# A 64-column rest unit in the first expert stage, and five moves around VectorE

## The chip, the cores and the metric

One core of a Trainium2 chip runs the kernel. Its TensorE (PE in the profile) multiplies, ScalarE (ACT) and VectorE (DVE) read PSUM and write SBUF, GpSimd (POOL) masks and scatters, SyncE (SP) issues most DMAs. The metric is the device time of one execution in microseconds; smaller is better.

## The reference

Decayed attention over 8 batches of 576 tokens, then two mixtures of experts, each of which sends every row to one of 8 experts:

```python
x = np.ascontiguousarray(attn_out.transpose(0, 2, 1, 3)).reshape(B * S, H * D)   # 4608 x 512
# both mixtures: e_idx = argmax(x @ w_gate [+ modality_bias])
for e in range(E):
    mask = e_idx == e
    h = np.maximum(x[mask] @ w1[e], 0.0)          # 512 -> 1024
    out[mask] = weight[mask, None] * (h @ w2[e])  # 1024 -> 512
```

Counting with the reference's own seeded inputs, the first mixture sends 602, 613, 589, 549, 586, 487, 608 and 574 rows to experts 0 to 7.

## The kernel before

The kernel has three parts. *Attention* (a written plan of times, `PLAN`, sorted and issued in that order) makes 36 chunks of 128 tokens, routes them, and scatters each row to its expert's place in DRAM. *Stage 1* walks the 8 experts of the first mixture in order, *stage 2* the 8 of the second. There each engine has its own stream of instructions with branches on register values, and the engines meet only at semaphores.

An expert's rows come in units. A pair unit has 256 rows, and alternates between slot 0 and slot 1; what is left over, up to 128 rows, is the *rest unit*. The number of pairs (`np`) and the kind of rest (`od`) are read from the row counts into registers of every engine. In stage 1 `od` is 0 (no rest) or 2 (a rest of 128 rows, though it may hold fewer); in stage 2 it can be 1, too, for a rest of at most 64 rows, which TensorE then multiplies with `SMALL`, 64 columns.

On TensorE a unit is the *first product* (`ph`, four quarters of 24 matmuls, lines 1136 to 1138, a weight load before each) and then, block of 128 rows by block, the *second product* (`py`, 24 matmuls of 512 columns a block, lines 1144 to 1146). The weights are two f16 numbers each, so each product is three. After each quarter of the first product ScalarE writes `max(ph, 0)` to `hT` in f16 (line 1264) and VectorE what f16 lost of it (the *rest of h*, line 1388); the second product takes `h_full` four times, once for each quarter. After the second product each block goes *back*: ScalarE squares `py` (1249), VectorE makes a scale from the sum (`eb`, `v_s`), ScalarE scales (1252), VectorE writes the low half of the row (`x2row`).

Between these lies the routing for the second mixture, some units late: TensorE makes logits (`L1114`), VectorE *chooses* (six small instructions from `w_L` to `oh`), TensorE counts ranks from `oh` (`L1119`, `L1120`; it waits for `oh_full`), VectorE *places* (`v_gq`, `w_pr`, `cum`). `routed` sets after which quarter each is done: in slot 0 a block is chosen at quarter 0 and its ranks are counted after quarter 2 of the first product, and another chosen at quarter 2 with its ranks after the first quarter of the second product.

The next expert's weights come as four staged megabytes; of each a `conv` on ScalarE (1238, about 1.9 us) makes the high half, and one on VectorE (`wb<-stg`, about 2.29 us) the low half. TensorE takes `w_full` for two of them before an expert's first product, for the other two before its second product in slot 0. For expert 1 the four are converted inside expert 0 and, the last on VectorE, in slot 0 of expert 1. VectorE's small work all has line 559, since one helper (`Chain`) issues it; each result that others wait for is told by waits that VectorE's sequencer runs one after another. `ahead` loads `np` and `od` of the next expert into the engine's registers.

Of the kernel before, what the change touches and what calls it, by code (L numbers as in the profile page):

```python
# [13 lines left out]
F32 = mybir.dt.float32  # L14
I32 = mybir.dt.int32
AF = mybir.ActivationFunctionType
ALU = mybir.AluOpType
# [75 lines left out]
def attention_and_routing(tc, st, I, K):  # L93
# [328 lines left out]

    def enough():

        pm = ps.tile([P, 512], F32, tag="pl", name="pm_enough")
        nc.tensor.matmul(pm[:, 0:8], ones, held[0], start=True, stop=True)
        nc.vector.tensor_copy(K["reg1"][:, 24:25], pm[0:1, 0:1])

# [40 lines left out]
    def counts():  # L469

        pm = total[0]
        cf = one.tile([1, 8], F32, tag="cf", name="cf")
        c2 = one.tile([1, 1, 8], I32, tag="c2", name="c2")
        reg = K["reg1"]
        nc.vector.tensor_copy(reg[:, 16:24], pm[0:1, 0:8])
        nc.vector.tensor_tensor(cf, pm[0:1, 0:8], col("eR")[0:1], op=ALU.subtract)
        nc.vector.tensor_scalar(c2[:, 0], cf, 127.0, None, op0=ALU.add)
        nc.vector.tensor_scalar(reg[:, 0:8], c2[:, 0], 8, None, op0=ALU.logical_shift_right)
        nc.vector.tensor_scalar(reg[:, 8:16], c2[:, 0], 6, 2, op0=ALU.logical_shift_right, op1=ALU.bitwise_and)


    fetch, high, low = first_weights(nc, I, K, lambda m: two.tile([P, 1024], F32, tag="w0s", bufs=4, name=f"w0s{m}"))
# [91 lines left out]
def experts(nc, st, I, K, out):  # L574
# [159 lines left out]
                unit(P_, 1, PAIR, True)  # L734
                eng.reg_add(i, i, 1)

    def walk(co, R_, P_, unit, none=None, conv=None, first=None, late=None, opening=None, owed=None):

        eng, pairs, od = co.eng, R_["np"][P_ % E], R_["od"][P_ % E]
        if P_ < E:  # L740
            block, after = co.label("block"), co.label("after")

            def without():
                if none:
                    none()
                if first and P_ == 0:
                    first()
                if owed:
                    owed()
                for k in range(2 if conv and P_ == 0 else 0):  # L750
                    conv(1, k)
                if conv and P_:
                    for slot in range(2):
                        for q in range(2):
                            brought(eng, R_, P_, conv, slot, q)

            def other():
                with when(eng, pairs, "GT", 1):
                    unit(P_, 1, PAIR, True, 1)
                    pairs_from(eng, R_, P_, unit, 2)  # L760
                if conv:
                    with eng.Else():
                        for k in range(2) if P_ == 0 else ():
                            conv(1, k)
                        for q in range(2) if P_ else ():
                            brought(eng, R_, P_, conv, 1, q)
            if opening and P_ == 0:
                opening(without)
            else:
                co.unlikely(pairs, "LT", 1, without, block)  # L770
                unit(P_, 0, PAIR, False, 0)
            co.unlikely(pairs, "NE", 2, other, block)
            unit(P_, 1, PAIR, True, 1)
            co.to(block)
            if late:
                co.unlikely(od, "EQ", 0, late, after)
            else:
                co.jump(od, "EQ", 0, after)
            unit(P_, 2, FULL, False)
            co.to(after)  # L780
            return
        with when(eng, pairs, "GT", 0):
            unit(P_, 0, PAIR, False, 0)
            with when(eng, pairs, "GT", 1):
                unit(P_, 1, PAIR, True, 1)
                pairs_from(eng, R_, P_, unit, 2)
        if none:
            with eng.Else():
                none()
        with when(eng, od, "EQ", 2):  # L790
            unit(P_, 2, FULL, False)
        with eng.Else():
            with when(eng, od, "EQ", 1):
                unit(P_, 2, SMALL, False)
        if conv:
            rest(eng, R_, P_, conv)
# [58 lines left out]
    with nc.Block() as block:  # L855
# [245 lines left out]
        def _(pe):  # L1101
            with ExitStack() as rs:
# [89 lines left out]
                for P_ in range(NP):  # L1192
                    if P_ == E:
                        take(pe, "w_full", 4)
                        with when(pe, R_["early"], "GT", 0):
                            for k in range(EP):
                                unit(E, k, PAIR, False, routing=k == 0, counting=k == 0)
                        with pe.Else():
                            routed(pe, was, 0, False, None, lambda b: (logits(b), ranks(b)))
                            counts(cum)  # L1200
                        take(pe, "reg_pe")
                        less_early(pe, R_)
                    co.leave(R_, P_)
                    if P_ and P_ != E:
                        take(pe, "w_full", 2)

                    def none(P_=P_):
                        if P_ not in (0, E):
                            take(pe, "w_full", 2)
                        coming(P_)  # L1210
                        if P_ == E - 2:
                            counts(cums)
                    def opening(without):

                        def slow():
                            count1(pe, R_, 0)
                            with when(pe, R_["np"][0], "LT", 1):
                                without()
                            with pe.Else():
                                ready(READY)  # L1220
                                unit(0, 0, PAIR, False, 0)
                        go = co.label("go")
                        co.unlikely(R_["known"], "LT", PAIR, slow, go)
                        unit(0, 0, PAIR, False, 0, made=True)
                        count1(pe, R_, 0)
                        co.to(go)
                    walk(co, R_, P_, unit, none, opening=opening)
                co.end()

        @block.scalar  # L1230
        def _(ac):
            with ExitStack() as rs:
# [24 lines left out]
                def unit(P_, s, w, sure, slot=None, routing=None):  # L1257
# [13 lines left out]
                    if opening:  # L1271
                        go = co.label("go")
                        co.unlikely(R_["known"], "LT", PAIR, relus, go)
                        co.to(go)
                    else:
                        relus()
                        if slot == 0:
                            brought(ac, R_, P_, conv, slot, 1)
                        for k in (2, 3) if (P_, s) == (0, 2) else ():
                            conv(1, k)  # L1280
                    ac.sem_inc(T[f"x_free{s}"])
                    for b in range(blocks[s]):
                        back(P_, s, b)
                    if P_ < E:
                        note(ac, was, s, sure)

# [4 lines left out]
                for P_ in range(NP):  # L1291
# [9 lines left out]
                        less_early(ac, R_)  # L1301
                    co.leave(R_, P_)
                    ahead(ac, R_, P_)
                    walk(co, R_, P_, unit, conv=conv, late=(lambda: [conv(1, k) for k in (2, 3)]) if P_ == 0 else None)
                co.end()

        @block.vector
        def _(ve):
            ch = Chain(ve, T, "dve")
            tt, ts, stt, tr = ve.tensor_tensor, ve.tensor_scalar, ve.scalar_tensor_tensor, ve.tensor_reduce  # L1310
            with ExitStack() as rs:
# [66 lines left out]
                def unit(P_, s, w, sure, slot=None, routing=None):  # L1378
# [3 lines left out]
                    def rests():  # L1382
                        for g in range(4):
                            routes = routing or behind(P_, slot)
                            if routes and g < 3:
                                routed(ve, was, s, sure, g, choose, 2)
                            take(ve, "hh_full")
                            stt(hT[:, 1, 2 * g:2 * g + 2, cs], ph[g][:, :, cs], 0.0, hT[:, 0, 2 * g:2 * g + 2, cs], op0=ALU.max, op1=ALU.subtract).then_inc(T["h_full"])  # L1388
                            if routes:
                                if g == 3:  # L1390
                                    routed(ve, was, s, sure, g, choose, 2)
                                if (P_, s, g) == (E - 2, 2, 3):
                                    order()
                                if (P_, s, g) == (0, 2, 3):
                                    conv(1, 2)
                                if slot == 0 and g == 3:
                                    brought(ve, R_, P_, conv, 0, 0)
                                routed(ve, was, s, sure, g, place, 2)
                            if P_ and slot == 1 and g == 1:
                                brought(ve, R_, P_, conv, slot, 0)  # L1400
                            if (P_, slot, g) == (0, 1, 1):
                                conv(1, 0)
                            if (P_, slot, g) == (1, 0, 1):
                                conv(1, 3)
                    if opening:
                        go = co.label("go")
                        co.unlikely(R_["known"], "LT", PAIR, rests, go)
# [80 lines left out]
                for P_ in range(NP):  # L1488
# [13 lines left out]
                            final_counts()  # L1502
                        less_early(ve, R_)
                    co.leave(R_, P_)
                    ahead(ve, R_, P_)

                    def none():
                        ve.sem_inc(T["cnt_ask"])
                        totals()
                    walk(co, R_, P_, unit, none if P_ == E - 2 else None, conv, nothing, {0: lambda: conv(1, 2), E - 2: order}.get(P_),  # L1510
                         owed=(lambda: conv(1, 3)) if P_ == 1 else None)
                co.end()

        @block.gpsimd
# [135 lines left out]
```

## Time and profile before

| | us |
|---|---|
| median of 3 runs | 987.47 (987.39 to 988.93) |
| the profiled execution | 986.25 |
| its span, first to last instruction | 984.5 |
| TensorE busy in it | 964.9 (98%) |
| VectorE, ScalarE busy | 437.1 (44%), 353.8 (36%) |

Busy is the time with at least one instruction in flight, so a share of 98% says that TensorE is seldom seen waiting, not that its array runs at its peak. Times in the rows count from the span's start. Attention lasts until about 181, stage 1 until 594, stage 2 to the end.

### The profile page before, as it was taken

To read this page: it belongs to the slowest core of one execution; us is meant where nothing else is said; L and a number is where in the kernel's file an instruction comes from. 1 tells how busy PE (TensorE), PEld (TensorE's weight loads), DVE (VectorE), ACT (ScalarE), POOL (GpSimd) and SP (SyncE) were. 2 spreads that over 40 slices of the span, in tenths; PEclk is the share of its full clock that TensorE was granted. 3 is DMA by queue.
4 is the path that set the end of the run, shared out by engine and by line. 5 is a ranking of instruction groups with operands and counts; after the bars stand their busy time and mean duration, and the time that the engine had idled before them with its cause. 6 is when DMAs were issued, how large, how long until landed. Compare 5 with 4: busy or idle time off the path is not lost. (4 is left out here: it accounts for less than half of the span.)

```text
span 984.5 us, 25261 instructions
## 1 busy us (share of the span) xinstructions
PE 964.9 (98%) x9218; PEld 684.2 (69%) x9218; DVE 437.1 (44%) x1402; ACT 353.8 (36%) x699; POOL 213.1 (22%) x301
## 2 busy tenths in 40 slices
PE   8999998999999999999999999999999999999997
PEld 6888887666676766767775776776666667766664
DVE  4676677366656565656566663243111211121111
ACT  4665565235444352434453432232111111211111
POOL 6677765011111111111111111100010101000110
PEclk9999999999999999999999999999999999999999
DMA  9999992578376664748664852642221311112101
GB/s 349 375 337 328 330 303 111 121 216 235 75 194 139 150 189 122 196 110 236 121 184 97 235 161 61 215 87 44 55 60 36 76 35 55 43 43 64 54 21 36
DMA packets 170070, 145.20 MB, mean 147 GB/s; under 512 B 135081, under 2 KB 135245, under 8 KB 169936
## 3 DMA queue, kind: packets, MB, share of 16 engines
q1 hardware_dynamic: 160928, 114.85, 43.0%
q0 software_dynamic: 8960, 28.62, 7.8%
q8 instruction: 73, 1.20, 0.5%
q14 instruction: 61, 0.50, 0.2%
q10 hardware_dynamic: 48, 0.04, 0.0%
HBM read 80.46 MB, written 33.92 MB: 116 GB/s over the span
## 5 line engine op out<-in xcount | busy, mean ns | idle before, releaser
L1138 PE MATMUL ph<-xT,wb 128*128 128x256 f16 (+2 forms) x1312 | 329.3, 262 | 0.0
L1137 PE MATMUL ph<-xT,wb 128*128 128x256 f16 (+2 forms) x1312 | 329.3, 262 | 0.0
L1136 PE MATMUL ph<-xT,wb 128*128 128x256 f16 (+2 forms) x1312 | 329.2, 262 | 0.0
L1388 DVE SCALAR_TENSOR_TENSOR hT<-ph,hT 128x512 f16<-128x512 f32 (+2 forms) x164 | 103.2, 636 | 322.0 <-DVEq L547 321.2
L1144 PE MATMUL py<-wb,hT 128*128 128x512 f16 x608 | 230.3, 379 | 0.1
L1146 PE MATMUL py<-wb,hT 128*128 128x512 f16 x608 | 230.4, 379 | 0.0
L1145 PE MATMUL py<-wb,hT 128*128 128x512 f16 x608 | 230.4, 379 | 0.0
L1264 ACT ACTIVATE hT<-ph 128x512 f16<-128x512 f32 (+2 forms) x164 | 90.1, 550 | 175.8 <-ACTq L547 175.6
L1136 PEld LDWEIGHTS ph<-xT,wb 128*128 128x128 f16 x1312 | 128.2, 98 | 15.6
L1137 PEld LDWEIGHTS ph<-xT,wb 128*128 128x128 f16 x1312 | 128.2, 98 | 15.4
L1138 PEld LDWEIGHTS ph<-xT,wb 128*128 128x128 f16 x1312 | 128.3, 98 | 12.2
L1146 PEld LDWEIGHTS py<-wb,hT 128*128 128x128 f16 x608 | 59.4, 98 | 71.8
L1551 POOL DMA_INDIRECT out_dram<-yo,idxo x37 | 35.9, 970 | 334.5 <-POOLq L547 324.7
L1144 PEld LDWEIGHTS py<-wb,hT 128*128 128x128 f16 x608 | 59.3, 98 | 64.3 <-issue 0.9
L1145 PEld LDWEIGHTS py<-wb,hT 128*128 128x128 f16 x608 | 59.4, 98 | 63.2
L559 DVE SCALAR_TENSOR_TENSOR wb<-stg,wb 128x2048 f16<-128x2048 f32 x36 | 82.4, 2288 | 10.0 <-DVEq L547 9.0
L1255 ACT ACTIVATE yo<-py,v_gcol 128x512 f32<-128x512 f32 x37 | 25.4, 687 | 167.5 <-ACTq L547 167.5
L1540 POOL TENSOR_SCALAR idx<-v_pos 128x1 int32<-128x1 f32 x39 | 9.1, 232 | 335.0 <-POOLq L547 335.0
L1238 ACT ACTIVATE wb<-stg 128x2048 f16<-128x2048 f32 x36 | 68.4, 1901 | 0.9 <-ACTq L547 0.9
L1249 ACT ACTIVATE sq<-py 128x512 bf16<-128x512 f32 x39 | 23.3, 596 | 93.4 <-ACTq L547 93.4
L1544 POOL DMA_INDIRECT xs<-x2row,idx x39 | 43.3, 1111 | 37.8 <-POOLq L547 36.5
L332 POOL TENSOR_SCALAR_AFFINE_SELECT a<-a 128x512 f32<-128x512 f32 x64 | 39.5, 641 | 26.2 <-ACT a L326 25.3
(165 smaller groups left out, 946.5 us busy)
## 6 DMA issues: line engine op xcount, KB each, us to landing
stg<-in_moe_w_dram SPq DMA_DIRECT2D x36, 1024.0 KB
dq<-in_dq_dram SPq DMA_DIRECT2D x34, 512.0 KB
vk<-in_vk_dram SPq DMA_DIRECT2D x30, 512.0 KB
w0s<-in_moe_w_dram SPq DMA_DIRECT2D x8, 512.0 KB
xs<-zero SPq DMA_DIRECT2D x8, 262.0 KB, 2.3
xs<-zero SPq DMA_DIRECT2D x8, 258.0 KB
vk<-in_vk_dram SPq DMA_DIRECT2D x8, 256.0 KB
gx<-in_scales_dram SPq DMA_DIRECT2D x5, 256.0 KB
```

The lines of the kernel that those rows point to most:

```text
L332: nc.gpsimd.affine_select(out=d4, in_=d4, pattern=[[0, 4], [1, C]], compare_op=ALU.is_ge, fill=0.0, base=0, channel_multiplier=-1)
L559: r = fn(*a, **kw).then_inc(self.sem, 1)
L1136: pe.matmul(o, w1(P_, 0)[:, c, fs], xT[s][:, c, cs], start=(c == 0), stop=False)
L1137: pe.matmul(o, w1(P_, 0)[:, c, fs], xT[s][:, 4 + c, cs], start=False, stop=False)
L1138: m = pe.matmul(o, w1(P_, 1)[:, c, fs], xT[s][:, c, cs], start=False, stop=(c == 3))
L1144: pe.matmul(py[b], hT[:, 0, f, bs], w2(P_, 0)[:, f, :], start=(f == 0), stop=False)
L1145: pe.matmul(py[b], hT[:, 0, f, bs], w2(P_, 1)[:, f, :], start=False, stop=False)
L1146: m = pe.matmul(py[b], hT[:, 1, f, bs], w2(P_, 0)[:, f, :], start=False, stop=(f == 7))
L1238: ac.activation(wb[P_ % 2][:, 0, 2048 * c:2048 * c + 2048], stg[:, 2048 * c:2048 * c + 2048], AF.Copy, scale=WS).then_inc(T["cv_full"])
L1264: ac.activation(hT[:, 0, 2 * g:2 * g + 2, cs], ph[g][:, :, cs], AF.Relu).then_inc(T["hh_full"])
L1388: stt(hT[:, 1, 2 * g:2 * g + 2, cs], ph[g][:, :, cs], 0.0, hT[:, 0, 2 * g:2 * g + 2, cs], op0=ALU.max, op1=ALU.subtract).then_inc(T["h_full"])
L1544: po.indirect_dma_start(out=xs2, out_offset=bass.IndirectOffsetOnAxis(ap=idx[b], axis=0), in_=x, in_offset=None, bounds_check=E * R - 1, o ...
```

## The change

Six edits:

1. `od` in stage 1 becomes 0, 1 or 2, and TensorE's walk gets a rest unit of 64 columns for `od` 1, laid out ahead of the 128-column one. The other engines still do all 128 columns. By the row counts, experts 3 (549 = 512 + 37) and 7 (574 = 512 + 62) have such a rest; 0, 1, 2, 4 and 6 have a longer one, 5 has none.
2. `pm_enough`, the small product in attention that tells early how many rows expert 0 has, moves from the PSUM buffer `pl` to the two that `px` rotates through.
3. Expert 1's third weight quarter is converted earlier: on ScalarE in slot 1 of expert 0, on VectorE ahead of the rest unit's choice.
4. Expert 1's fourth quarter is converted on VectorE at quarter 0 of slot 0 instead of quarter 1.
5. VectorE's `ahead` of experts 1 to 7 moves from the expert's start behind the choice at quarter 0 of slot 0.
6. In slot 1 of expert 6 VectorE's first conversion moves from behind quarter 1 to behind the choice at quarter 2.

```diff
-        pm = ps.tile([P, 512], F32, tag="pl", name="pm_enough")
+        pm = ps.tile([P, 512], F32, tag="px", bufs=2, name="pm_enough")
...
-        nc.vector.tensor_scalar(reg[:, 8:16], c2[:, 0], 6, 2, op0=ALU.logical_shift_right, op1=ALU.bitwise_and)
+        nc.vector.tensor_scalar(c2[:, 0], c2[:, 0], 6, 3, op0=ALU.logical_shift_right, op1=ALU.bitwise_and)
+        nc.vector.tensor_scalar(reg[:, 8:16], c2[:, 0], 1.0, 1.0, op0=ALU.max, op1=ALU.subtract)
... (walk, TensorE only: short=True)
-            co.to(block)
+            if short:
+                co.jump(od, "EQ", 0, after)
+                co.jump(od, "EQ", 2, block)
+                unit(P_, 2, SMALL, False)
+                eng.br(after)
+                co.at(block)
+            else:
+                co.to(block)
... (ScalarE, unit)
-                        for k in (2, 3) if (P_, s) == (0, 2) else ():
-                            conv(1, k)
+                        if (P_, s) == (0, 2):
+                            conv(1, 3)
                     for b in range(blocks[s]):
                         back(P_, s, b)
+                        if (P_, slot, b) == (0, 1, 0):
+                            conv(1, 2)
... (VectorE, rests, for each quarter g)
+                            if slot == 0 and g == 0 and 0 < P_ < E:
+                                ahead(ve, R_, P_)
+                            if (P_, slot, g) == (1, 0, 0):
+                                conv(1, 3)
+                            if (P_, slot, g) == (E - 2, 1, 2):
+                                brought(ve, R_, P_, conv, slot, 0)
                             take(ve, "hh_full")
...
                             if routes:
+                                if (P_, s, g) == (0, 2, 3):
+                                    conv(1, 2)
                                 if g == 3:
                                     routed(ve, was, s, sure, g, choose, 2)
-                                if (P_, s, g) == (0, 2, 3):
-                                    conv(1, 2)
...
-                            if P_ and slot == 1 and g == 1:
+                            if P_ not in (0, E - 2) and slot == 1 and g == 1:
                                 brought(ve, R_, P_, conv, slot, 0)
-                            if (P_, slot, g) == (1, 0, 1):
-                                conv(1, 3)
```

VectorE in the rest unit of expert 0, from the last rest of h on (`wb1` is expert 1's weights, `w_L0` to `oh20` the choice of block 0, `v_gq0` begins its placing). Before:

```order
L1388 SCALAR_TENSOR_TENSOR hT<-ph3,hT 128x2x128
L559 TENSOR_REDUCE w_L0<-pr0 128x8
L559 SCALAR_TENSOR_TENSOR w_l20<-w_L0,v_inv20,cur0 128x8
L559 TENSOR_REDUCE v_mx0<-w_l20 128x1
L559 SCALAR_TENSOR_TENSOR w_w0<-w_l20,v_mx0,cst 128x8
L559 TENSOR_REDUCE v_m20<-w_w0 128x1
L559 TENSOR_SCALAR oh20<-w_w0,v_m20,cur0 128x8
L559 SCALAR_TENSOR_TENSOR wb1<-stg,wb1 128x2048
L559 SCALAR_TENSOR_TENSOR v_gq0<-v_sume0,v_rinv20 128x1
```

After:

```order
L1406 SCALAR_TENSOR_TENSOR hT<-ph3,hT 128x2x128
L560 SCALAR_TENSOR_TENSOR wb1<-stg,wb1 128x2048
L560 TENSOR_REDUCE w_L0<-pr0 128x8
L560 SCALAR_TENSOR_TENSOR w_l20<-w_L0,v_inv20,cur0 128x8
L560 TENSOR_REDUCE v_mx0<-w_l20 128x1
L560 SCALAR_TENSOR_TENSOR w_w0<-w_l20,v_mx0,cst 128x8
L560 TENSOR_REDUCE v_m20<-w_w0 128x1
L560 TENSOR_SCALAR oh20<-w_w0,v_m20,cur0 128x8
L560 SCALAR_TENSOR_TENSOR v_gq0<-v_sume0,v_rinv20 128x1
```

The conversion went from behind the choice to ahead of it.

VectorE at the start of expert 1, to its first rest of h (`w_L1` to `oh21` is the choice of block 1, the two loads are `ahead`). Before:

```order
L625 TENSOR_LOAD reg1
L626 TENSOR_LOAD reg1
L669 COMPARE_AND_BRANCH
L648 COMPARE_AND_BRANCH
L559 TENSOR_REDUCE w_L1<-pr1 128x8
L559 SCALAR_TENSOR_TENSOR w_l21<-w_L1,v_inv21,cur1 128x8
L559 TENSOR_REDUCE v_mx1<-w_l21 128x1
L559 SCALAR_TENSOR_TENSOR w_w1<-w_l21,v_mx1,cst 128x8
L559 TENSOR_REDUCE v_m21<-w_w1 128x1
L559 TENSOR_SCALAR oh21<-w_w1,v_m21,cur1 128x8
L822 UNCONDITIONAL_BRANCH
L1388 SCALAR_TENSOR_TENSOR hT<-ph0,hT 128x512
```

After:

```order
L649 COMPARE_AND_BRANCH
L560 TENSOR_REDUCE w_L1<-pr1 128x8
L560 SCALAR_TENSOR_TENSOR w_l21<-w_L1,v_inv21,cur1 128x8
L560 TENSOR_REDUCE v_mx1<-w_l21 128x1
L560 SCALAR_TENSOR_TENSOR w_w1<-w_l21,v_mx1,cst 128x8
L560 TENSOR_REDUCE v_m21<-w_w1 128x1
L560 TENSOR_SCALAR oh21<-w_w1,v_m21,cur1 128x8
L832 UNCONDITIONAL_BRANCH
L626 TENSOR_LOAD reg1
L627 TENSOR_LOAD reg1
L560 SCALAR_TENSOR_TENSOR wb1<-stg,wb1 128x2048
L1406 SCALAR_TENSOR_TENSOR hT<-ph0,hT 128x512
```

The loads went behind the choice, and the fourth conversion, which stood behind the second rest of h, went ahead of the first.

TensorE in attention, behind `pm_enough` (`px` is a chunk turned, `pl` its gate logits; in brackets whose semaphore an instruction waits for). Before:

```order
L351 MATMUL px_0_2506<-idf,og_0_2476 128x2x64 [waits DVE_49]
L351 MATMUL px_0_2506<-idf,og_0_2476 128x2x64 x3
L354 MATMUL pl_0_2507<-cst,og_0_2476 64x16 [waits DVE_49]
L354 MATMUL pl_0_2507<-cst,og_0_2476 64x16 x7
L316 MATMUL po_1_2522<-dq_1_2069,Sb_100 64x128 x8
```

After:

```order
L351 MATMUL px_0_2506<-idf,og_0_2476 128x2x64 [waits DVE_49,PE_49]
L351 MATMUL px_0_2506<-idf,og_0_2476 128x2x64 x3
L354 MATMUL pl_0_2507<-cst,og_0_2476 64x16 [waits PE_49]
L354 MATMUL pl_0_2507<-cst,og_0_2476 64x16 x7
L316 MATMUL po_1_2522<-dq_1_2069,Sb_100 64x128 [waits PE_49]
```

Line 354 no longer waits for VectorE; line 351 does, as before, but in the built program for VectorE's 272nd update instead of its 265th. The 265th is `og` (line 344) of the chunk that is turned, the 272nd is `xr` (line 379), the last reader of the `px` before, and the 273rd, for which line 354 waited, is the copy of `pm_enough` (line 427).

## Rows read from the trace of the kernel before

**Rows 1.** The page, section 1: engine, busy us, share, instructions.

```profile
PE 964.9 (98%) x9218; PEld 684.2 (69%) x9218; DVE 437.1 (44%) x1402; ACT 353.8 (36%) x699; POOL 213.1 (22%) x301
```

**Rows 2.** Stretches: us; PE, PEld, DVE, ACT, POOL busy; PEclk; DMA share; GB/s.

```profile
224.57:250.31 25.74, 23.61 (x168) 15.25 (x167) 17.17 (x46) 10.97 (x19) 5.78 (x9) 0.93 0.74 213
303.78:325.12 21.34, 21.34 (x165) 14.58 (x164) 13.49 (x41) 9.73 (x18) 2.78 (x6) 1.00 0.40 87
507.01:529.63 22.62, 21.63 (x166) 14.61 (x165) 15.48 (x43) 9.60 (x18) 3.44 (x7) 1.00 0.38 86
235.95:239.36 3.41, 3.27 (x16) 2.03 (x15) 2.91 (x3) 1.01 (x1) 2.41 (x2) 0.50 1.01 389
```

**Rows 3.** TensorE alone, three first products: of 256, 128 and 64 columns.

```profile
335.92:346.85 10.93, 10.93 (x118) 1.00 0.83 263
378.60:383.96 5.36, 5.36 (x98) 1.00 0.45 106
782.05:784.85 2.80, 2.80 (x97) 1.00 0.04 10
```

**Rows 4.** Timeline (start, us, engine, instruction, idle before): expert 3's rest unit, VectorE.

```profile
382.75 1.12 DVE L1388 SCALAR_TENSOR_TENSOR hT<-ph,hT 128x256 f16<-128x256 f32 x3 [0.68 <-DVEq L547]
```

**Rows 5.** TensorE early in attention: timeline, then a stretch.

```profile
7.93 1.16 PE L287 MATMUL pa<-dq 64*128 64x128 f32 x16 [2.15 <-DMA dq<-in_dq_dram]
...
7.70:12.00 4.30, 4.07 (x54) 2.94 (x54) 1.29 (x7) 1.47 (x3) 3.43 (x5) 1.00 1.03 387
```

**Rows 6.** Timeline, VectorE, from expert 0's rest into expert 1.

```profile
219.96 0.43 DVE L1388 SCALAR_TENSOR_TENSOR hT<-ph,hT 128x256 f16<-128x256 f32 x1 [0.53 <-DVEq L547]
...
224.42 2.29 DVE L559 SCALAR_TENSOR_TENSOR wb<-stg,wb 128x2048 f16<-128x2048 f32 x1 [1.94 <-DVEq L547]
...
229.62 0.74 DVE L559 SCALAR_TENSOR_TENSOR x2row<-py,v_s,x2row 128x512 f16<-128x512 f32 x1
232.66 0.18 DVE L559 TENSOR_REDUCE w_L<-pr 128x8 f32<-128x24 f32 x1 [2.30 <-DVEq L547]
...
234.57 0.69 DVE L1388 SCALAR_TENSOR_TENSOR hT<-ph,hT 128x512 f16<-128x512 f32 x1 [0.38 <-DVEq L547]
...
235.97 0.69 DVE L1388 SCALAR_TENSOR_TENSOR hT<-ph,hT 128x512 f16<-128x512 f32 x1 [0.48 <-DVEq L547]
236.58 2.28 DVE L559 SCALAR_TENSOR_TENSOR wb<-stg,wb 128x2048 f16<-128x2048 f32 x1
239.34 0.18 DVE L559 TENSOR_REDUCE w_L<-pr 128x8 f32<-128x24 f32 x1 [0.48 <-DVEq L547]
...
240.60 0.29 DVE L559 TENSOR_SCALAR oh<-w_w,v_m,cur 128x8 f16<-128x8 f32 x1
```

**Rows 7.** Timeline, ScalarE in expert 0's rest unit.

```profile
222.38 3.69 ACT L1238 ACTIVATE wb<-stg 128x2048 f16<-128x2048 f32 x2
225.97 0.57 ACT L1249 ACTIVATE sq<-py 128x512 bf16<-128x512 f32 x1
```

**Rows 8.** Timeline, TensorE: the ranks in expert 1 slot 0.

```profile
234.40 0.17 PE L1119 MATMUL pr<-oh,tri 128*128 128x8 f16 x1 [1.60 <-PEq L547]
...
241.09 0.17 PE L1119 MATMUL pr<-oh,tri 128*128 128x8 f16 x1 [0.27 <-PEq L547]
```

**Rows 9.** VectorE's loads of `np`: shortest, median, longest, in ns.

```profile
L625 DVEq TENSOR_LOAD <-reg x8: 305/660/716, 181.8 to 490.1; - x8
```

**Rows 10.** Timeline, TensorE and VectorE: expert 6 slot 1.

```profile
524.38 0.17 PE L1119 MATMUL pr<-oh,tri 128*128 128x8 f16 x1
...
523.77 0.33 DVE L559 TENSOR_SCALAR oh<-w_w,v_m,cur 128x8 f16<-128x8 f32 x1
```

**Rows 11.** Timeline, TensorE and VectorE: attention behind `pm_enough`.

```profile
129.33 0.66 PE L351 MATMUL px<-idf,og 128*128 128x128 f32 x4
130.61 0.64 PE L354 MATMUL pl<-cst,og 128*64 128x16 f32 x16 [0.62 <-DVE reg L427]
...
129.76 0.74 DVE L379 SCALAR_TENSOR_TENSOR xr<-px,sc,xr 128x512 f16<-128x512 f32 x1
```

More of the change, by code (lines that the diff above doesn't have):

```diff
@@ L735, in pairs_from, with walk @@
                 eng.reg_add(i, i, 1)
-    def walk(co, R_, P_, unit, none=None, conv=None, first=None, late=None, opening=None, owed=None):
+    def walk(co, R_, P_, unit, none=None, conv=None, first=None, late=None, opening=None, owed=None, ready=2, short=False, later=None):
         eng, pairs, od = co.eng, R_["np"][P_ % E], R_["od"][P_ % E]
@@ L743, in without @@
             def without():
+                if later:
+                    later()
                 if none:
@@ L749, in without @@
                     owed()
-                for k in range(2 if conv and P_ == 0 else 0):
+                for k in range(ready if conv and P_ == 0 else 0):
                     conv(1, k)
@@ L762, in other @@
                     with eng.Else():
-                        for k in range(2) if P_ == 0 else ():
+                        for k in range(ready) if P_ == 0 else ():
                             conv(1, k)
@@ L1226, in opening @@
                         co.to(go)
-                    walk(co, R_, P_, unit, none, opening=opening)
+                    walk(co, R_, P_, unit, none, opening=opening, short=True)
                 co.end()
@@ L1303, in _ @@
                     ahead(ac, R_, P_)
-                    walk(co, R_, P_, unit, conv=conv, late=(lambda: [conv(1, k) for k in (2, 3)]) if P_ == 0 else None)
+                    walk(co, R_, P_, unit, conv=conv, late=(lambda: conv(1, 3)) if P_ == 0 else None, ready=3)
                 co.end()
@@ L1504, in _ @@
                     co.leave(R_, P_)
-                    ahead(ve, R_, P_)
+                    if P_ in (0, *range(E, NP)):
+                        ahead(ve, R_, P_)
                     def none():
@@ L1510, in _ @@
                     walk(co, R_, P_, unit, none if P_ == E - 2 else None, conv, nothing, {0: lambda: conv(1, 2), E - 2: order}.get(P_),
-                         owed=(lambda: conv(1, 3)) if P_ == 1 else None)
+                         owed=(lambda: conv(1, 3)) if P_ == 1 else None,
+                         later=(lambda P_=P_: ahead(ve, R_, P_)) if 0 < P_ < E else None)
                 co.end()
```

## The prediction

> **What bounds the kernel now.** I read the page first, then the pace of TensorE by stretches, then the timelines of the places that the diff touches. TensorE is busy in 98% of the span [rows 1], so the kernel is TensorE's own work plus the few places where it is held up, and an edit counts only for what it does to that engine. A pair unit without a hold-up is 21.34 us long (expert 2 slot 1, the second row), expert 1 slot 0 (the first) 25.74 and expert 6 slot 1 (the third) 22.62 [rows 2]: 4.40 and 1.28 us could be won there. [...] A pause of 2.15 us early in attention, between small products, left the clock at 1.00 [rows 5], and so did what makes up the 1.28 us in expert 6. [...]
>
> **Edit 1, the short rest unit.** The first product takes 5.36 us at 128 columns and 2.80 at 64 [rows 3]: 2.56 us less of TensorE's work in each of experts 3 and 7. But the second product takes the rest of h, which VectorE still makes for 128 columns, and VectorE begins it in expert 3 at 382.75, after 0.68 us of waiting [rows 4]; what stands before that on VectorE belongs to the previous unit, which doesn't change. Three pieces take 1.12, so the first is done at about 383.17, and TensorE can go on at about 383.27. Today its second product starts at 383.96 [rows 3]. The unit gets shorter by 0.7, not by 2.56; TensorE ends its first product at 378.60 + 2.80 = 381.40 and then stands 1.87 us. Expert 7 has the same work around it, so I take two times −0.7 = −1.4. The bounds are two times −2.56 = −5.1, if VectorE can start earlier, and 0. [...]
>
> The trace says how the matmul's time goes with its columns: 96 matmuls in 5.36 us and in 2.80 us, 56 and 29 ns each [rows 3]. [...]
>
> **Edit 2, `pm_enough` in `px`.** Line 354 loses a wait of 0.62 [rows 11], but by the order line 351 of the next chunk now needs `px` free, that is `xr` of the chunk before, which ends at 129.76 + 0.74 = 130.50 [rows 11]. Line 351 started at 129.33 and would start at 130.56; its 0.66 is then done at about 131.2, where line 354 started at 130.61. Behind it on TensorE is the rest of attention, with little slack for some time: +0.5. Bounds: 0, if a later wait of attention swallows it, and +0.75, if line 316's new wait costs a little too.
>
> **Edits 3 to 5, around expert 1.** VectorE, not TensorE, sets the end of this stretch, so I follow VectorE. Before: the last rest of h ends at 220.39, a choice, the third conversion from 224.42 to 226.71, placing, `x2row` at 229.62 to 230.36, then 2.30 idle with the two loads in it, and the next choice from 232.66 [rows 6]. After: the conversion is ahead of the choice, from about 220.3 to 222.6; the choice takes 1.55 (as from 239.34 to 240.89 [rows 6]) and ends at 224.65 with its steps, so expert 1 begins on TensorE at 224.85, 0.3 later than now. ScalarE converts only one quarter in the rest unit, but behind the same gate, so its square (225.97 before [rows 7]) comes at about 226.3. The back work behind it no longer has 2.29 of conversion in its way: I put the end of `x2row` at 229.3, 1 earlier. The next choice, without loads ahead of it, runs from 230.2 to 231.75, and TensorE, which needs it at 234.40 − 1.60 = 232.80 [rows 8], no longer waits there.
>
> Then comes what was moved. Two loads at the median of 0.66 are 1.3 [rows 9], the fourth conversion 2.29 [rows 6], and with about 1.0 of waits between (two of the 0.48 that stand before such work [rows 6]) the first rest of h starts at 236.4, where it was 234.57. TensorE's first product ends at 224.87 + 10.93 = 235.8 [rows 3] and now waits 1.3 for it. The second rest of h comes 1.40 later [rows 6], then the other choice (1.55), and the ranks are counted at 240.14 instead of 241.09 [rows 8]: −0.95, say −1.0. With both loads at the shortest 0.305 [rows 9] it would be −1.7; with 1 us more on VectorE's path nothing is won, so the bounds are −1.7 and 0. The stall goes, but the conversion, now ahead of what the second product needs, is late in its place.
>
> The clock comes on top. Today's half-clock stretch lies ahead of the wait at 241.09 and is partly hidden by it: VectorE would have been late anyway. After the change TensorE stands 1.3 us for the first rest of h and 1.7 us more before the rank count; a fall now comes at the end of this, with nothing left to hide it. Between 0 and 1.7, I take +1.0, since the pauses are together longer than the one that cost the clock before. Expert 1 then gives 0 in all.
>
> **Edit 6, expert 6 slot 1.** VectorE is busy before the choice, which ends at 523.77 + 0.33 = 524.10, and TensorE counts ranks at 524.38 [rows 10]. The conversion and the choice are both still ahead of that; moving one past the other moves the pause from one quarter to the next. I take 0, with bounds −0.4 and +0.1 by the nearest gap (0.28 between 524.10 and 524.38).
>
> The larger program (a second kind of rest unit with its branches in all eight experts) I cost at 0: experts are walked in line today, with jumps between them, and no row shows a price for it.
>
> **The sum.** Attention +0.5, expert 1 −1.0, short units −1.4, expert 6 0: −1.9 at full clock. With +1.0 of clock in expert 1 and one of the two short units followed by a half clock (+1.7), it is +0.8. Against the profiled execution, 986.25, that is 987.05; the median of the runs shown is 987.47, 1.22 above the profile, and I take the sum to the median: 988.3.
>
> **Rivals.**
> *The clock holds.* It held through 2.15 us [rows 5], against it is the fall after 1.60 [rows 2, 8]. Then the sum is −1.9: 985.6.
> *The clock falls at all three places* (other side). The condition is that a pause of 1.6 amid dense work is enough: the short units stand 1.87 each, expert 1 stands 3.0 in two pauses. The price is 1.70 in each: +0.5 −1.0 −1.4 + 3 × 1.7 = +2.2, or 989.7. For it speaks that the only such pause in stage 1 was followed by a fall; against it expert 6.
> *VectorE isn't the bound.* If the pauses in expert 1 and 6 are only a matter of the order, and the first rest of h in the short units follows TensorE, all is won: −5.1 −4.4 −1.3 +0.5 = −10.3, or 977.2. Against it is VectorE's unbroken row of work in rows 6; for it only that the 0.68 before the rest of h [rows 4] is a wait and not work.
> *The short unit does nothing.* If 64 columns go no faster beside the expert's other traffic, edit 1 is worth 0, and with expert 1 at 0 too, 988.0.
>
> **How the numbers follow.** About 0.2% (2 us) is what a measurement of this kernel can tell from no change. The forecast, with gains and clock cancelling, has 0.50; its own range is 986.4 to 989.6 (attention 0 to 0.75, no fall or a whole one more or less in the short units), so 0.04 of it lie on the faster side, 0.42 within, 0.04 slower. The clock holds: 0.16, half of it faster. Three falls: 0.20, with 0.13 slower and 0.07 within. VectorE not the bound: 0.09, faster. The short unit does nothing: 0.05, within. Together 0.21, 0.61 and 0.18. The range from 985.0 to 990.3 leaves out the third rival and the tails of the first two, less than 2 in 10.
>
> **What the changed profile would show.** Right: line 351 at about 130.5 behind an idle stretch and line 354 without a wait; expert 1 slot 0 without a wait at its first rank count, with one before its second product, and about 25 long; in the rests of experts 3 and 7 a first product of 2.80, then an idle stretch of about 1.9 in front of the second product; expert 6 slot 1 still near 22.6; VectorE's loads right behind the choice. Half clock would stand as stretches of 0.50 behind these pauses. Wrong: a second product in expert 3's rest right behind its first, VectorE's first rest of h there well before 4 us after the first product starts (382.75 − 378.60 = 4.15 today), expert 1 slot 0 near 21.3, or a new hold-up somewhere that the diff does not touch.

## The result, and the profile after

| | before | after |
|---|---|---|
| median | 987.43 (985.85 to 988.93, 6 runs) | 996.36 (993.49 to 999.13, 6 runs) |
| ratio, with 95% interval | | 1.0088 (1.0073 to 1.0103) |
| profiled execution, its span | 986.25, 984.5 | 994.07, 992.3 |

The changed kernel is slower by 8.9 us, where +0.8 was forecast; the range ended at 990.3.

The page of the changed kernel, sections 1 and 3 (the second: queue, packets, MB, share of 16 engines):

```profile
PE 962.6 (97%) x9218; PEld 680.2 (69%) x9218; DVE 437.1 (44%) x1403; ACT 353.5 (36%) x699; POOL 213.4 (22%) x301
...
q8 instruction: 80, 1.31, 0.6%
q14 instruction: 62, 0.51, 0.2%
```

The same rows of the page of before:

```profile
q8 instruction: 73, 1.20, 0.5%
q14 instruction: 61, 0.50, 0.2%
```

TensorE runs as many matmuls as before and is busy 2.3 us less [rows 1]; the span is 7.8 longer, so it waits 10.1 us more. VectorE's one instruction more is the second line of `od` in edit 1. The other count that grew is that of the packets of kind "instruction", in which, as I read the name, program text is brought: in q8 80 of 16 KB each (1.31 MB), where there were 73.

Where the 7.8 us lie is read off the starts of TensorE's first products in the two timelines. The stretches that aren't listed differ by 0.04 at most.

| stretch on TensorE | before | after | difference |
|---|---|---|---|
| to the start of stage 1 | 181.46 | 182.32 | +0.86 |
| expert 0 slots 0 and 1 | 32.32 | 32.17 | −0.15 |
| expert 0 rest | 10.79 | 11.73 | +0.94 |
| expert 1 slot 0 | 25.74 | 23.03 | −2.71 |
| expert 3 rest | 10.80 | 10.16 | −0.64 |
| expert 4 slot 0 | 21.34 | 27.20 | +5.86 |
| expert 5 (two units, no rest) | 42.77 | 43.67 | +0.90 |
| expert 7 slot 0 | 21.40 | 21.83 | +0.43 |
| expert 7 rest | 10.80 | 13.40 | +2.60 |
| stage 2 | 390.54 | 390.28 | −0.26 |

Not every row is the change's work. Expert 7 slot 0 is 21.84 in dead_short below, which has none of the moves and runs no short unit, and the start of stage 1 lies anywhere from 180.34 to 184.24 in the profiles of this document.

Stretches of the changed kernel, columns as in [rows 2]: expert 1 slot 0, expert 3's rest, expert 4 slot 0, expert 6 slot 1, expert 7's rest.

```profile
226.22:249.25 23.03, 21.60 (x164) 14.57 (x165) 14.81 (x41) 10.47 (x19) 3.69 (x7) 1.00 0.74 212
377.55:387.70 10.15, 8.39 (x131) 5.46 (x130) 5.21 (x19) 3.07 (x10) 0.00 (x0) 1.00 0.64 129
387.70:414.91 27.21, 23.17 (x168) 15.37 (x166) 12.83 (x43) 9.71 (x18) 6.15 (x9) 0.94 0.63 196
512.08:534.70 22.62, 22.03 (x167) 14.36 (x166) 15.87 (x43) 9.49 (x18) 3.26 (x7) 1.00 0.37 89
588.66:602.06 13.40, 8.54 (x131) 5.54 (x130) 7.08 (x29) 4.44 (x13) 1.39 (x3) 1.00 0.39 81
```

Three things came as worked out: expert 1 slot 0 has lost its first stall, expert 3's short unit is 0.64 shorter, expert 6 slot 1 is unchanged. The two that hurt lie right behind the short units, where the diff leaves the order of work alone. TensorE's timeline there, at the start of expert 4 and then at the end of expert 7 (start, us, instruction, idle before and its releaser):

```profile
387.70 0.27 PE L1146 MATMUL ph<-xT,wb 128*128 128x256 f16 x1
387.81 0.27 PE L1147 MATMUL ph<-xT,wb 128*128 128x256 f16 x1
387.92 0.27 PE L1148 MATMUL ph<-xT,wb 128*128 128x256 f16 x1
392.23 0.27 PE L1146 MATMUL ph<-xT,wb 128*128 128x256 f16 x1 [4.04 <-issue]
...
598.78 0.17 PE L1130 MATMUL pr<-cum,ones 128*128 128x8 f16 x1
602.06 0.27 PE L1146 MATMUL ph<-xT,wb 128*128 128x256 f16 x1 [3.11 <-PEq L548]
```

The first pause stands between two matmuls of one quarter, which wait for nothing, and its releaser is "issue", the page's word for a wait that it can't explain. The second carries the name of a wait instruction, for `w_full`. In the trace's sequencer records that wait stands at 601.67 with 0.05 us. Its length tells nothing, since a real wait stands with 0.05 us at its end, too (that for VectorE's rest of h, at 382.16). But the last conversion had told `w_full` at 589.56, twelve us before, and TensorE's sequencer ran nothing at all from 598.78 to 601.67. The same holds before expert 6, where `w_full` had been told at 477.61 and the wait stands at 490.32. So I read all three pauses as the next instructions not being there. The trace has the times of the 16 KB packets in q8:

```
                  last instruction   packet came (start + us)   next instruction
expert 4 begins        387.92           390.06 + 0.95               392.23
expert 6 begins        489.51           487.89 + 0.88               490.32
expert 7 ends          598.78           599.15 + 1.05               601.67
```

The code that was asked for lies behind a jump over the 128-column unit, which the short path has to leave out. That TensorE stands there until a packet has come is my reading; no record names what it waits for. The pause behind expert 7, of 3.3 us, fits it: nothing behind the jump had run. The one in expert 4, of 4.2 us, fits only in part: three matmuls behind the jump's target had run before TensorE stood. Before expert 6 the packet had ended before TensorE ran out of work, and still nothing ran until 1.55 us behind its end. In the experiments below such pauses stand only in kernels with the added block and its jumps.

After the first of them the granted clock was at 0.50 for 3.41 us (its stretch of 27.21 has 0.94 on average): 4.2 + 1.7 = 5.9 is the +5.86 of the table.

### The profile page after: what moved, and what is told of

Same layout as the page of the kernel before. It is cut to its first block, busy times and chain, and to the rows that moved or that the text cites. A ratio compares the mean times of both kernels' runs of the same rounds, so it can differ in the third digit from the quotient of the medians.

```text
span 992.3 us, 25278 instructions
## 1 busy us (share of the span) xinstructions
PE 962.6 (97%) x9218; PEld 680.2 (69%) x9218; DVE 437.1 (44%) x1403; ACT 353.5 (36%) x699; POOL 213.4 (22%) x301
## 3 DMA queue, kind: packets, MB, share of 16 engines
q8 instruction: 80, 1.31, 0.6%
## 5 line engine op out<-in xcount | busy, mean ns | idle before, releaser
L1146 PE MATMUL ph<-xT,wb 128*128 128x256 f16 (+2 forms) x1312 | 324.3, 261 | 8.6 <-PEq L548 4.5
L1148 PE MATMUL ph<-xT,wb 128*128 128x256 f16 (+2 forms) x1312 | 324.4, 261 | 0.0
L1147 PE MATMUL ph<-xT,wb 128*128 128x256 f16 (+2 forms) x1312 | 324.3, 261 | 0.0
```

The source lines that it names most:

```text
L1146: pe.matmul(o, w1(P_, 0)[:, c, fs], xT[s][:, c, cs], start=(c == 0), stop=False)
L1147: pe.matmul(o, w1(P_, 0)[:, c, fs], xT[s][:, 4 + c, cs], start=False, stop=False)
L1148: m = pe.matmul(o, w1(P_, 1)[:, c, fs], xT[s][:, c, cs], start=False, stop=(c == 3))
```

## The experiments

Ratios are against runs of the kernel before on the same chip, whose medians were 985.5 to 986.5 there. The expected times count from 987.4, so a ratio is held against them as that ratio times 987.4.

**no_short**: the changed kernel, edit 1 undone.

```diff
-                    walk(co, R_, P_, unit, none, opening=opening, short=True)
+                    walk(co, R_, P_, unit, none, opening=opening)
```

(and `od` by its old line)

> The changed kernel without edit 1 (no 64-column rest unit in TensorE's stage 1, the kind of rest 0 or 2 as before); edits 2 to 6 stay. Theory A, the added program: the loss comes from TensorE standing while its own program is brought, behind the added block. Then the pauses after expert 3 (4.2 us and the half clock behind it), before stage 2 (3.2) and before expert 6 (1.0) are gone; attention stays 0.9 later, expert 1 slot 0 stays about 2 to 2.7 shorter: 985 to 987. Theory B, the moved conversions and loads (edits 3 to 6) make experts start late: stays near 995. Theory C, the short unit's own pauses of 1.9 us and the clock behind them: near 986 too, so this run tells B from A and C.

Measured 984.46, ratio 0.9986 (0.9974 to 0.9998). Expert 4 slot 0 is 21.34 long, expert 7's rest 10.80, expert 5 42.68. All the loss belongs to edit 1, and edits 2 to 6 win a little (the interval ends just below 1): theory B falls.

**short_only**: the kernel before with edit 1 alone.

```diff
+            if short:
+                co.jump(od, "EQ", 0, after)
+                co.jump(od, "EQ", 2, block)
+                unit(P_, 2, SMALL, False)
+                eng.br(after)
+                co.at(block)
...
+        nc.vector.tensor_scalar(reg[:, 8:16], c2[:, 0], 1.0, 1.0, op0=ALU.max, op1=ALU.subtract)
```

> The kernel before with edit 1 alone. Theory A (program): the pauses of 3 to 4 us behind the short units of experts 3 and 7 are there with no other edit, and the sum is about +8 to +11 with 1.3 won inside the units: 994 to 998. Theory B (moved conversions and loads): 986 to 987, by 0.65 won twice. Theory C (pauses of 1.9 in the short units and half clock): at most 2 x 1.7 lost, 986 to 990.

Measured 994.83, ratio 1.0097 (1.0073 to 1.0121). TensorE's timeline at the same two places:

```profile
392.25 0.37 PE L1145 MATMUL ph<-xT,wb 128*128 128x256 f16 x1 [4.17 <-issue]
...
593.14 0.38 PE L1152 MATMUL py<-wb,hT 128*128 128x512 f16 x1 [1.97 <-PEq L548]
601.89 0.27 PE L1144 MATMUL ph<-xT,wb 128*128 128x256 f16 x1 [1.59 <-PEq L548]
```

Edit 1 alone makes the pauses behind both short units. The second is 1.7 us and not 3 to 4, as I had expected; its packet came earlier, from 598.70 to 600.01, when TensorE still worked (until 600.13). Here the clock also fell behind the pause of 1.97 us inside expert 7's short unit: the granted clock is 0.88 on average from 588.20 to 601.89.

**dead_short**: the kernel before with the block in TensorE's program, but `od` by its old line, so it is 0 or 2 and the block never runs.

> The kernel before with the block of the short unit in TensorE's program, but the kind of rest stays 0 or 2, so the block is jumped over by every expert and never run. Theory A (program): skipping costs something by itself, least where a rest unit follows (TensorE still has 5 us of first product queued behind the jump?), most where two blocks are skipped, before expert 6 (1 us); the big pauses behind experts 3 and 7 depend on what is jumped over there and may stay or go: 988 to 993. Theory C (the short unit's own running): as before, 987.4. Theory B: 987.4.

Measured 987.6, ratio 1.0012 (0.9997 to 1.0027). The page has 81 packets in q8 and 61 in q14: only TensorE's program had grown, and q8 had 73 before, so TensorE's text comes in q8. Expert 4 slot 0 (21.34) and expert 7's rest (10.79) are undisturbed. The new pause is before expert 6, where expert 5 jumps over both blocks:

```profile
488.97 0.27 PE L1143 MATMUL ph<-xT,wb 128*128 128x256 f16 x1 [1.36 <-PEq L547]
```

So a longer program by itself costs nothing that shows, and the jump over the short block doesn't either: at the rests of experts 0 to 4, 6 and 7 the gap behind the slot 1 unit is 0.22 as before. Not every jump over a block stalled; the one over two blocks did (1.36), and so did, in the changed kernel (4.2 and 3.3) and in short_only (4.2 and 1.7), the one over the 128-column block behind a short unit.

**in_place**: edits 2 to 6, and the 64-column unit instead of the 128-column one in experts 3 and 7, with no block or jump added. It can't do a longer rest there, which this data doesn't have.

```diff
-            unit(P_, 2, FULL, False)
+            unit(P_, 2, SMALL if co.tag == "pe" and P_ in (3, 7) else FULL, False)
```

(and edit 1 undone as in no_short)

> The changed kernel with the 64-column rest unit standing in the place of the 128-column one in experts 3 and 7, and nowhere else, so that TensorE's program gets no added block and no added jump (it can't do a longer rest in these two experts, which these row counts don't have). Theory A (program): the short units are worth their 0.65 each, no pause behind them, no half clock: 1.3 below the run without edit 1, 984 to 985.5. Theory C (pauses in the short units, clock): the pause of 1.9 before the second product stays and the clock falls behind one or both: 987 to 990.

Measured 981.79, ratio 0.9961 (0.9950 to 0.9972). The page has 73 packets in q8 again. Expert 3's rest and the start of expert 4, stretch by stretch, and the wait inside the short unit:

```profile
375.37:385.52 10.15, 8.39 (x131) 5.47 (x130) 5.21 (x19) 3.06 (x10) 0.00 (x0) 1.00 0.63 132
385.52:406.86 21.34, 21.34 (x168) 14.55 (x166) 12.75 (x43) 9.81 (x18) 4.15 (x9) 1.00 0.80 245
```

```profile
380.09 0.38 PE L1153 MATMUL py<-wb,hT 128*128 128x512 f16 x1 [1.76 <-PEq L547]
```

The same 64-column unit with the same wait for VectorE, and neither a pause behind it nor a half clock: theory C falls, and the unit is worth its 0.65 in the trace as soon as it brings no jump. By the medians this kernel is 2.7 us faster than no_short, where two units of 0.65 give 1.3; the rest isn't explained.

**moved_128**: the changed kernel with 128 instructions that are jumped over, ahead of expert 0 in TensorE's program.

```diff
+                go = co.label("go")
+                co.jump(was, "EQ", 0, go)
+                for _ in range(128):
+                    pe.reg_mov(was, 0)
+                co.to(go)
```

> The changed kernel with 128 instructions that are jumped over put in front of expert 0 in TensorE's program, so that all that follows lies elsewhere in the 16 KB packets in which it is brought; no semaphore, no order of work and no duration changes. Theory A: the pauses behind experts 3 and 7 and before expert 6 change size, each anywhere between 0 and 5 us, and so does the total: 988 to 1000. Any theory in which they come from waits between engines: the same pauses, 996 (with up to 1 us for the new jump).

Measured 992.15, ratio 1.0055 (1.0034 to 1.0076). The pause behind expert 7 is gone, those at expert 4 and before expert 6 stay, and a new one of 0.5 us stands within the first product of expert 2's rest. Stretch and timeline:

```profile
589.95:600.10 10.15, 8.40 (x132) 5.46 (x131) 5.30 (x19) 3.07 (x10) 0.00 (x0) 1.00 0.46 85
```

```profile
326.46 0.23 PE L1148 MATMUL ph<-xT,wb 128*128 128x128 f16 x1 [0.36 <-issue]
...
392.22 0.37 PE L1148 MATMUL ph<-xT,wb 128*128 128x256 f16 x1 [3.86 <-issue]
```

No semaphore and no order of work differ from the changed kernel's, and 3.3 us went as the code moved, so I put the pause down to where the code lies and not to a wait between engines. Here q8's packet came at 593.30, while the short unit was still running, and not at 599.15 behind it. The intervals of the two ratios overlap a little, so it is the two profiles that carry this, one of each kernel.

**short_first**: the changed kernel, but the branch holds only the first product; the second is shared.

```diff
+                    elif pick:
...
+                        co_.jump(od, "EQ", 2, whole)
+                        first(cols(P_, SMALL))
+                        pe.br(joined)
+                        co_.at(whole)
+                        first()
+                        co_.to(joined)
```

> The changed kernel, but the branch takes in only the first product: 64 or 128 columns, then one second product for both. The added block is about four fifths of the short unit's, and what the short path jumps over comes before a place where TensorE waits 1.9 us for VectorE anyway. Theory A (program): skipping still costs little where the jump lies under the slot 1 unit's work, and behind the short first product the pause grows from 1.9 to 3 or 4 in place of the 4.2 and 3.3 behind the unit, so 4 to 8 us less than the changed kernel: 987 to 992. If the pauses behind experts 3 and 7 were anything but the jump over the block, they would stay at the start of the next expert: 996.

Measured 985.85, ratio 1.0005 (0.9990 to 1.0021): by the ratios 8 us less than the changed kernel, and like the kernel before. Experts 3 and 7 have rests of 10.15 and 10.14, with the same 1.92 before the second product as in place; I had expected that pause to grow. The jump goes over some four fifths of what it went over before, and TensorE waits 1.9 us behind it anyway. By the trace the wait covers the packet in expert 3: it came from 380.88 to 382.07, TensorE's last matmul of the first product started at 382.22, the first instruction behind the jump ran at 383.54, and VectorE's rest of h was there at 384.06. In expert 7 the code was there already: that instruction ran at 587.94, before the first product's last matmul (588.02). The code lies elsewhere here too, which in moved_128 took one pause away by itself; so how much of the 8 us is due to the sharing isn't shown. The pause that remains is the one before expert 6:

```profile
487.19 0.27 PE L1139 MATMUL ph<-xT,wb 128*128 128x256 f16 x1 [0.88 <-PEq L548]
```

**moves_only** (edits 3 to 6), and **best** (edits 3 to 6 with the 64 columns in place).

> The kernel before with edits 3 to 6 alone (no short unit, the early count in its old buffer). Expert 1 slot 0 loses 2.7 us, the boundary before it gains 0.9 (the choice now ends later than the rest unit, and the steps of TensorE's queue behind the rank count are no longer covered), expert 6 stays: about -1.8 without the 0.5 of edit 2, ratio 0.998. If edit 2 were the useful one, it would be above the run that had it.

> Edits 3 to 6, and the 64-column rest unit in the place of the 128-column one in experts 3 and 7 alone (it can't do a longer rest there, which these row counts don't have). Theory A (added program is the only loss of edit 1): -1.8 - 1.3 = -3.1, ratio 0.997, faster than both kernels, and no pause behind experts 3 and 7. If edit 2 gains in attention, this is slower than the same kernel with edit 2 (0.9961).

Measured 984.21, ratio 0.9984 (0.9975 to 0.9993), and 982.64, ratio 0.9968 (0.9956 to 0.9981). Both are faster than the two kernels; edit 2 makes no difference that these runs can tell (0.9986 with it, 0.9984 without; in place 0.9961 with it, 0.9968 without).

**choice_first**: best, with VectorE's conversion behind the choice again.

```diff
-                                if (P_, s, g) == (0, 2, 3):
-                                    conv(1, 2)
                                 if g == 3:
                                     routed(ve, was, s, sure, g, choose, 2)
...
+                                if (P_, s, g) == (0, 2, 3):
+                                    conv(1, 2)
```

> Edits 3 to 6 and the 64-column unit in place, but VectorE's conversion of expert 1's third quarter goes back behind the choice in expert 0's rest unit (half of edit 3 undone). If VectorE's row of work sets the end of expert 1 slot 0 whatever its order, the 0.9 us that TensorE waits before expert 1 goes, and comes back as waiting inside expert 1 slot 0, whose end stays where it is: ratio 0.997, as with the conversion ahead. If the order does matter, the boundary's 0.9 is won on top: ratio 0.996. If the back work behind the conversion comes later (the placing and the scale stand behind it), the first rank count of expert 1 waits again, by up to 1 us: ratio 0.998.

Measured 982.67, ratio 0.9959 (0.9943 to 0.9975), not to be told from best. Expert 0's rest is 10.79 instead of 11.63, expert 1 slot 0 23.49 instead of 23.12: of the 0.84 won before the expert, 0.37 come back as waiting inside it.

## Why the prediction was wrong

**The step that failed** is the one sentence "The larger program (a second kind of rest unit with its branches in all eight experts) I cost at 0: experts are walked in line today, with jumps between them, and no row shows a price for it." It should have had a bound, like the other unknown costs. In stage 1 of before, no jump leads over a whole unit to work that is needed at once except after expert 5, and there it was free (from the last matmul of expert 5, at 485.43, to the first of expert 6, at 485.64, it is 0.21 us, as between two matmuls of the second product); I took that for all jumps. Measured: 4.2 us behind expert 3 with 1.7 of half clock, 3.3 behind expert 7, about 1.0 before expert 6. Together that is some 10 us, more than the 7.8 by which the span grew. Without it the sum would be −2.3, and I had −1.9 at full clock.

**Edit 1, the unit itself: right.** VectorE's first rest of h came at 381.70 (4.15 after the unit's start, as before), the second product at 382.27:

```profile
381.70 1.45 DVE L1406 SCALAR_TENSOR_TENSOR hT<-ph,hT 128x256 f16<-128x256 f32 x4 [0.68 <-DVEq L548]
```

TensorE stood 1.9 us, as worked out, and the unit shrank by 0.64 (−0.7 predicted), not by 2.56. The half clock that I put behind one of these two pauses came in none of the two here, and in 1 of the 14 short units of all kernels above. It came with all three pauses of 4.0 to 4.3 (here, short_only, moved_128: a granted clock of 0.94, 0.94 and 0.88 over expert 4 slot 0), and not behind the 3.3 of expert 7 (1.00). The 1.7 is half of the 3.41 us at 0.50 in [rows 2]. No run but short_only shows such a price in a short unit: about 1.6 there (13.69 us at 0.88), and 0 in the other 13.

**Edit 2: about right in place, not measurable in the whole.** Line 351 waited 1.25 us and began at 130.86 (predicted 130.56), and line 354 followed without a wait:

```profile
130.86 0.63 PE L351 MATMUL px<-idf,og 128*128 128x128 f32 x4 [1.25 <-DVE reg L427]
131.42 0.35 PE L354 MATMUL pl<-cst,og 128*64 128x16 f32 x6
```

From `pm_enough` to line 316 it is 3.65 us instead of 3.06, so +0.6. Stage 1 started at 180.34 to 184.24 in the profiles with this edit and at 180.72 to 183.77 in those without; this hides half a microsecond. What I left out is the clock: in three of the five profiles with this edit (no_short, moved_128, short_first) it was at 0.50 for 3.41 us from 131.8 to 133.4 on, some 2 us behind the end of this wait, and in none of the six without it near this place. From `pm_enough` to line 448 those three took 41.8 to 42.3 us, the two others with the edit 40.2 and 40.6.

**Edits 3 to 5: the steps along VectorE were right, three sizes were not.** The first rank count of expert 1 no longer waits; the first rest of h started at 236.26 (236.4 predicted), the second count was at 240.04 (240.14), though all of stage 1 ran 0.7 late by then. So the times agree by luck; counted from the start of expert 0's rest, both came 0.8 earlier than worked out:

```profile
236.26 0.69 DVE L1406 SCALAR_TENSOR_TENSOR hT<-ph,hT 128x512 f16<-128x512 f32 x1 [0.49 <-DVEq L548]
```

```profile
225.54 0.17 PE L1130 MATMUL pr<-cum,ones 128*128 128x8 f16 x1
226.22 0.27 PE L1146 MATMUL ph<-xT,wb 128*128 128x256 f16 x1 [0.51 <-PEq L548]
...
240.04 0.17 PE L1129 MATMUL pr<-oh,tri 128*128 128x8 f16 x1 [1.43 <-PEq L548]
```

Three sizes were off. The two moved loads took 0.32 and 0.30 us, where I had taken the median of 0.66 each [rows 9]; that is 0.7 of the 0.8. All the loads of `np` in the changed kernel:

```profile
L626 DVEq TENSOR_LOAD <-reg x8: 301/313/543, 182.6 to 494.5; - x8
```

At experts 1 to 5 a load took 0.30 to 0.32 us in each of the eight kernels with edit 5, and 0.58 to 0.74 in the three without. A load got shorter by being moved; why, no run shows. Second, expert 1 began 0.94 later instead of 0.3, since the choice now ends after TensorE's rest unit, and the waits and branches between two experts (0.68 us, from 225.54 to 226.22) are no longer covered by matmuls. With both, no wait stood before the second product, where I had put 1.3: the first product ended at 237.15, behind the first rest of h, and the slot is 23.03 long, not about 25. Third, no half clock came behind the 1.43 (the granted clock is 1.00 over the slot here, as in best and choice_first), so the +1.0 for it was wrong. From the start of expert 0's rest to the end of expert 1 slot 0 it is 34.76 instead of 36.53, −1.77 us, where I had −1.0 before the clock, with a bound of −1.7 for loads at their shortest. That the fall in [rows 2] had cost nothing by itself is seen in dead_short and short_only, which had none there and were as long (25.78 and 25.81).

**Edit 6: right.** Expert 6 slot 1 is 22.62 in both kernels.

Of the rivals, only "the clock falls at all three places" forecast a loss that a measurement can tell, for another reason and at other places. Its sum is miscounted: +0.5 −1.0 −1.4 + 5.1 is +3.2, or 990.7, and not +2.2, so it lay outside my range. The chances by side add up to 0.21, 0.62 and 0.17, where 0.61 and 0.18 stand. The rival that was missing is a jump behind which TensorE stands (4.2, 3.3 and about 1.0 us here), as I read it because the program isn't there yet.

## What to carry to other kernels

A path that is added to a program brings jumps, and here three of them cost 4.2, 3.3 and about 1.0 us that no order of instructions showed; keep the two paths' difference small and share what they have in common (short_first, with its shared second product, won back 8 us here). When a timeline shows a pause between two instructions of one loop that wait for nothing, or a wait whose semaphore had been told long before, compare the packet counts of the instruction queues and move the code without changing it; if the pause goes, as the 3.3 us behind expert 7 did in moved_128, suspect where the code lies before any wait between engines. A cost that no row shows is unknown and not 0, and it needs a bound as wide as the nearest thing that the trace does show.

## What was not expected of the hardware

The pauses are of 0.5 to 4.3 us with packets that take 0.9 to 1.6. One part is steady: in all eleven pauses of this kind (three in the changed kernel, three in moved_128, two each in short_only and short_first, one in dead_short) the next instruction ran 1.2 to 1.6 us behind the end of a q8 packet. So these pauses are long or short by when the packet starts: 2.1 us behind the last instruction in expert 4 (a pause of 4.2), 1.6 before it at expert 6 (about 1.0). What sets that stays open, and so does why the jump over one block was free ahead of a 128-column unit (a gap of 0.22 in dead_short) and not behind a short one; moved_128 shows only that a move of the code takes part in it (no pause behind expert 7 instead of 3.3). Nor is it settled why the granted clock fell for 6.83 us and not 3.41 in moved_128. The loop seen here pays nothing: from 723.5 to 788.1 us, in a loop of stage 2 over pair units, q8 has no packet in the changed kernel, and TensorE is busy all the time.
